# Half of each w3 and w_out block moved from the sync queue to ScalarE's queue

## The chip, the cores and the metric

The kernel runs on one NeuronCore of a Trainium2 chip. Five engines work side by side, each through its own instructions in order: TensorE (PE, matrix products), VectorE (DVE), ScalarE (ACT), GpSimd (POOL) and SyncE (SP). SP computes nothing here; it issues transfers between the device memory and the core's own memory. ScalarE can issue such transfers too, as instructions among its computing ones. The engines meet only at semaphores: an instruction that needs another engine's result, or a transfer's, waits for a count, and everything behind it on its own engine waits with it.

The metric is the device time of one execution in microseconds (us). The median of three runs of the kernel before is 259.25 us (258.74 to 259.34).

## The reference

Attention with a polynomial sketch (4 batches, 4 heads, 1088 positions, 32 dimensions, sketch size 8) feeds a multiplicative feed-forward block over 4352 tokens of width 128 with 1024 inner columns. All inputs are float64.

```python
def phi(x):
    a = np.einsum('rd,bhsd->bhsr', S1, x)
    b = np.einsum('rd,bhsd->bhsr', S2, x)
    return np.einsum('bhsi,bhsj->bhsij', a, b).reshape(*x.shape[:-1], r * r)
q_p, k_p = (phi(q), phi(k))
kv = np.einsum('bhsf,bhsd->bhfd', k_p, v)
z = np.sum(k_p, axis=2)
num = np.einsum('bhsf,bhfd->bhsd', q_p, kv)
den = np.einsum('bhsf,bhf->bhs', q_p, z)[..., None] + 1e-06
x = (num / den).transpose(0, 2, 1, 3).reshape(B * S, H * D)
a = x @ w1
b = x @ w2
out = (a * b @ w3) @ w_out
```

## The kernel before, in words

The tokens are worked in eight groups of 512 (g0 to g7, two to a batch) and a rest of 256 (gr). For each group the queries are sketched and multiplied with the batch's key and value sums; the result is xT, a tile of 128 x 512. The feed-forward block then runs over eight chunks c of the inner 1024 columns: a product with w1 into the bank a_ps (step g.ca, line 1432), a copy of it by ScalarE into ffa (g.cc, line 1437), a product with w2 into b_ps (g.cb, line 1442), VectorE's product ab of the two (g.cm, line 1448), and the product of ab with w3o, summed over the chunks into ps_o (g.co, line 1455).

w3 and w_out are folded first: w3o = w3 @ w_out, in eight row blocks of 128 (steps f0 to f7, lines 465 to 477). The float64 words are turned into float32 on the core. The weights come in eleven blocks, steps w0 to w10: w0 and w1 hold w1 and w2, w2 is all of w_out, w3 to w10 are the eight row blocks of w3. Each has the steps

- load (line 386): 1 MB of raw words into one of three raw buffers; for w2 to w10 in four transfers of 256 KB, quarter t filling partitions 32t to 32t + 31;
- m and c (lines 421 and 226 by way of the helper top_of): two passes of ScalarE over all 128 partitions of the raw tile, so each block's first pass needs all four quarters;
- j (line 434, VectorE) and a (line 439, GpSimd or VectorE): the two halves are joined.

A row block is then transposed (f.t, line 467, VectorE), multiplied with w_out (f.m, line 473, TensorE) and copied into w3o (f.o, line 477, ScalarE).

The order of all steps is written out by hand in the string ORDER, lines 59 to 112. Each engine's instructions are chained in that order (lines 1514 to 1518), so a step's place in the string fixes what stands ahead of it on the engine that carries it out. The engines run asynchronously: SP, which only issues, can be far ahead of the others in the string, held only by its semaphores. A load waits until its raw buffer has been read by ScalarE. Each transfer also signals one of eight completion counters, which are taken in turn, so a transfer waits until the one eight places earlier has landed.

The buffers of each kind are assigned by hand (SLOTS). The eight banks of the kind "b" are shared by the matrix products; a product into a bank waits until the bank's last reader is done.

Places in ORDER of some of the loads (each line is a piece of the string):

```python
q0.pc0 q0.p12 k1.kT0 q0.dn k1.rest0 q0.pt1 warm10 w3.load q0.de k0.kvm
...
q1.xT g0.3a w2.load k1.kp1 q3.max w4.load w2.m w2.c g0.1c
...
w9.m w9.c g1.7m g1.1m v1.loadr q2.p12 q2.dn w8.load v1.load
...
q3.C1 q2.de w5.load q2.rc q2.bs k1.kvc g0.7c q3.At g0.7m k1.kqt f3.m q3.Ct f3.o k1.kq w5.m
...
f2.o w10.load w10.m w7.c
```

In the first, q0.pc0 is a pT copy of ScalarE. In the last, the conversion w10.m is the very next step behind w10.load.

Of the kernel before, what the change touches and what calls it, by code (L numbers as in the profile page):

```python
# [45 lines left out]
WARM = [6] + [2] * 10 + [1] * 24  # L46

BY_PE = ()

POOL = set("""  # L50
    k0.Nf k0.Nh k0.rest1 k1.kp0 k1.kp1 k2.kp0 k3.kp0 q0.p12 q0.phi0 q1.al q1.p12 q1.p2 q2.p12 q2.p2
# [63 lines left out]
def bview(t, free):  # L115
    return bass.AP(tensor=t.tensor, offset=t.offset, ap=[list(t.ap[0])] + [list(d) for d in free])


def make_steps(ctx, tc, q, k, v, S1, S2, moe_w1, moe_w2, moe_w3, moe_w_out, out):
    nc = tc.nc  # L120
    dve, act, pe, pool, sp = nc.vector, nc.scalar, nc.tensor, nc.gpsimd, nc.sync
    B, H, S, D = q.shape
# [15 lines left out]
    def step(name):  # L138
        def keep(f):
            assert name not in steps, name  # L140
            steps[name] = f
            return f
        return keep

    def on(name):
        return pool if name in POOL else act if name in ACTS else dve
# [10 lines left out]
    def sb(tag, shape, dtype=F32, bufs=1, name=None):  # L157
        return place(work, tag, shape, dtype, bufs, name or tag)
# [66 lines left out]
    def top_of(dst, hi):  # L225
        act.activation(dst, hi.bitcast(F32), ACT.Prelu, scale=2.0 ** -112, alpha=-2.0 ** 32)  # L226
# [153 lines left out]
    raw, w3c, w3T = {}, {}, {}  # L380
    NW = 3 + NC

    def conv(n):
        x = {}

        @step(f"w{n}.load")
        def _():
            raw[n] = sb("raw", [128, 1024], I64)
            if n < 2:
                for i, w in enumerate((moe_w1, moe_w2)):  # L390
                    sp.dma_start(raw[n][:, i * 512:(i + 1) * 512], w[:, n * 512:(n + 1) * 512])
            elif n == 2:
                for t in range(4):
                    sp.dma_start(raw[n][t * 32:(t + 1) * 32],
                                 bass.AP(tensor=moe_w_out.tensor, offset=moe_w_out.offset + t * 256 * DM,
                                         ap=[[DM, 32], [32 * DM, NC], [1, DM]]))
            elif n - 3 in BY_PE:
                sp.dma_start(raw[n], moe_w3[(n - 3) * 128:(n - 2) * 128])
            else:
                for t in range(4):  # L400
                    sp.dma_start(raw[n][t * 32:(t + 1) * 32],
                                 bass.AP(tensor=moe_w3.tensor, offset=moe_w3.offset + (n - 3) * 128 * DF + t * 256,
                                         ap=[[DF, 32], [32 * DF, 4], [1, 256]]))


        def shape(x, by, turn):
            if n - 3 not in BY_PE:
                return bview(x, [[by, 1024]])
            return bview(x, [[(32 if turn else 256) * by, 4], [(128 if turn else 32) * by, 8], [by, 32]])

        words = lambda i: shape(raw[n].bitcast(I32)[:, i:], 2, False)

        @step(f"w{n}.c")
        def _():
            x["c"] = sb("cv_c", [128, 1024], bufs=2)
            top_of(shape(x["c"], 1, True), words(1))

        @step(f"w{n}.m")
        def _():
            x["m"] = sb("cv_m", [128, 1024], I32, bufs=2)  # L420
            act.mul(shape(x["m"], 1, True), words(0).bitcast(U32), 2.0 ** -29)  # L421

        def made():
            if n < 2:
                x["d"] = w12[:, n].rearrange("p i c -> p (i c)")
            elif n == 2:
                x["d"] = wo.rearrange("p c d -> p (c d)")
            else:
                x["d"] = w3c[n - 3] = sb("w3c", [128, 1024], bufs=2)
            return x["d"].bitcast(I32)  # L430

        @step(f"w{n}.j")
        def _():
            on(f"w{n}.j").tensor_scalar(made(), x["c"].bitcast(I32), 3, None, ALU.logical_shift_left)  # L434

        @step(f"w{n}.a")
        def _():
            d = x["d"].bitcast(I32)
            on(f"w{n}.a").tensor_tensor(d, d, x["m"], ALU.add)  # L439
# [6 lines left out]
    def fold(ko):  # L446
        t = {}

        if ko in BY_PE:
            for half in range(2):  # L450
# [37 lines left out]
    def rest_ap(src, b):  # L488
        return bass.AP(tensor=src.tensor, offset=(b * H * S + SM) * D, ap=[[D, SR], [S * D, H], [1, D]])

    def k_loads(b):
        @step(f"k{b}.zero")
        def _():
            k_sb[b] = sb("k", [128, H, NK, D], bufs=2)
            pool.memset(k_sb[b][other(b), :, NJ], 0.0)

        def main(heads):
            h0, n = heads
            (act if b == 0 else sp).dma_start(bview(k_sb[b][:, h0], [[NK * D, n], [1, NJ * D]]),
                          bass.AP(tensor=k.tensor, offset=(b * H + h0) * S * D,  # L500
                                  ap=[[NJ * D, 128], [S * D, n], [1, NJ * D]]))

        if b == 0:
            for i in range(2):
                step(f"k{b}.load{i}")(lambda i=i: main((2 * i, 2)))
        else:
            step(f"k{b}.load")(lambda: main((0, H)))

        @step(f"k{b}.loadr")
        def _():  # L510
            sp.dma_start(k_sb[b][own(b), :, NJ], rest_ap(k, b))

        @step(f"v{b}.zero")
        def _():
            v_sb[b] = sb("v", [128, H, NK, D], bufs=2)
            pool.memset(v_sb[b][other(b), :, NJ], 0.0)

        @step(f"v{b}.load")
        def _():
            if b == 0:  # L520
                sp.dma_start(bview(v_sb[b], [[NK * D, H], [1, NJ * D]]),
                             bass.AP(tensor=v.tensor, offset=b * H * S * D,
                                     ap=[[NJ * D, 128], [S * D, H], [1, NJ * D]]))
            else:
                for t in range(4):
                    sp.dma_start(bview(v_sb[b][t * 32:(t + 1) * 32], [[NK * D, H], [1, NJ * D]]),
                                 bass.AP(tensor=v.tensor, offset=b * H * S * D + t * NJ * D,
                                         ap=[[32 * D, 32], [S * D, H], [1, NJ * D]]))

        @step(f"v{b}.loadr")  # L530
        def _():
            sp.dma_start(v_sb[b][own(b), :, NJ], rest_ap(v, b))

        if b:
            @step(f"kh{b}.load")
            def _():
                n = 32 * D
                k_by[b] = sb("kh", [128, n])
                for h in range(H):
                    sp.dma_start(k_by[b][h * 32:(h + 1) * 32],  # L540
                                 bass.AP(tensor=k.tensor, offset=(b * H + h) * S * D, ap=[[n, 32], [1, n]]))

# [1006 lines left out]
```

## Time and profile before

| | |
|---|---|
| median of three runs | 259.25 us |
| the profiled execution | 260.99 us, span 259.2 us |
| TensorE busy | 249.1 us, 96% |
| VectorE busy | 163.8 us, 63% |
| ScalarE busy | 97.1 us, 37% |
| GpSimd busy | 62.4 us, 24% |
| transfers issued | 120 on SP, 2 on ScalarE (the first k loads) |
| w3 blocks | 32 transfers of 256 KB, median 6.9 us from issue to landing |
| w_out | 4 transfers of 256 KB, median 7.9 us |

The span is the time from the first to the last instruction that the profile shows; what lies around it belongs to the execution's own time. Busy times are sums over the span; a stage in which an engine never rests can hide in a low share. "Idle before" in a row is the time for which the engine waited ahead of that row, and the name behind the arrow is what ended the wait. A product in float32 is shown as two instructions, so "x2" is one tile.

### The profile page before, as it was taken

The page shows a single profiled execution, that of the slowest core. Times are in us where ns is not written, and L with a number is a line of the kernel's source. Part 1 is how long each engine was busy: PE and PEld are TensorE (multiplying, and loading weights), DVE is VectorE, ACT ScalarE, POOL GpSimd, SP SyncE. Part 2 cuts the span into 40 slices and gives each one's busy share as a digit, 9 for nine tenths or more (in the row PEclk, how much of TensorE's full clock was granted, in tenths as well). Part 3 has the DMA queues.
Part 4 walks back from the last instruction along what each step waited for, and adds up shares of the span by engine and source line. Part 5 has one row for each costly group of instructions (what it writes and reads, how often), then busy time and mean ns, then how long its engine had stood idle before and what let it go on. Part 6 is the DMA issues. An engine that isn't in the chain of part 4 may idle for free.

```text
span 259.2 us, 5896 instructions
## 1 busy us (share of the span) xinstructions
PE 249.1 (96%) x2457; PEld 136.8 (53%) x2457; DVE 163.8 (63%) x360; ACT 97.1 (37%) x182; POOL 62.4 (24%) x88
## 2 busy tenths in 40 slices
PE   2989999999999899999999999999999999999995
PEld 0667864456564454676455444544444445455554
DVE  3769799798989986997895966241414533341430
ACT  2765476956445590312233337221031201031000
POOL 3523426490436408303520050000001000000000
PEclk9979999999999999999999999999999999999999
DMA  6997499956949963003000001600020000010035
GB/s 184 299 271 181 143 217 215 230 111 147 210 114 230 214 175 81 3 0 90 1 3 3 0 3 29 97 1 0 1 39 0 3 0 0 10 31 3 0 52 90
DMA packets 32314, 22.53 MB, mean 87 GB/s; under 512 B 21408, under 2 KB 26784, under 8 KB 32288
## 3 DMA queue, kind: packets, MB, share of 16 engines
q1 hardware_dynamic: 31744, 21.64, 37.2%
q10 hardware_dynamic: 544, 0.52, 0.6%
q8 instruction: 19, 0.31, 0.5%
q14 instruction: 7, 0.06, 0.1%
HBM read 19.93 MB, written 2.23 MB: 85 GB/s over the span
## 4 chain that ended last, share of the span: by engine, by line
PE 89%; DVE 5%; DMA 2%; SPq 1%; issue 0%
PE b_ps L1442 22%; PE ps_o L1455 21%; PE a_ps L1432 21%; PE ps_w3o L473 6%; PE idle_ps L218 4%; DMA k<-in_k_dram 2%; PE ps_g L599 2%; PE ps_ac L1278 2%; PE ps_x L1392 2%; PE ps_kv L698 2%; PE ps_or L1462 1%; PE ps_ab L642 1%; DVE RC L167 1%; DVE ab L1448 1%; DVE q_m L177 1%; PE ps_xt L1179 1%
## 5 line engine op out<-in xcount | busy, mean ns | idle before, releaser
L1448 DVE TENSOR_TENSOR ab<-ffa,b_ps 128x512 f32<-128x512 f32 (+1 forms) x72 | 44.6, 645 | 48.9 <-PE b_ps L1442 41.9
L1437 ACT COPY ffa<-a_ps 128x512 f32<-128x512 f32 (+1 forms) x72 | 38.5, 565 | 84.4 <-PE a_ps L1432 81.3
L1442 PE MATMUL b_ps<-xT,w 128*128 128x512 f32 (+1 forms) x144 | 67.0, 569 | 0.0
L1432 PE MATMUL a_ps<-xT,w 128*128 128x512 f32 (+1 forms) x144 | 65.2, 568 | 0.0
L1455 PE MATMUL ps_o<-ab,w3o 128*128 128x512 f32 x128 | 61.3, 592 | 0.0
L1432 PEld LDWEIGHTS a_ps<-xT,w 128*128 128x128 f32 x144 | 27.0, 190 | 29.5 <-issue 24.9
L1442 PEld LDWEIGHTS b_ps<-xT,w 128*128 128x128 f32 x144 | 26.9, 190 | 28.9 <-issue 24.2
L1455 PEld LDWEIGHTS ps_o<-ab,w3o 128*128 128x128 f32 x128 | 24.0, 190 | 24.7 <-issue 23.2
L439 POOL TENSOR_TENSOR w3c<-w3c,cv_m 128x1024 int32<-128x1024 int32 x8 | 19.1, 2386 | 26.4 <-DVE w3c L434 15.0
L218 PE MATMUL idle_ps<-zeros 128*128 128x512 bf16 x50 | 16.0, 428 | 4.8 <-DVE zeros L190 4.8
L1373 POOL TENSOR_TENSOR ph<-s_al,s_bs 128x1024 f32<-128x1024 f32 (+1 forms) x5 | 9.9, 1990 | 43.6 <-DVE s_bs L1363 43.6
L473 PEld LDWEIGHTS ps_w3o<-wo,w3T 128*128 128x128 f32 x128 | 15.2, 192 | 4.5 <-DVE w3T L467 2.1
L473 PE MATMUL ps_w3o<-wo,w3T 128*128 128x128 f32 x128 | 15.5, 276 | 1.3 <-DVE w3T L467 1.3
L1471 DVE STREAM_TRANSPOSE oT<-ps_o 128x512 f32<-128x512 f32 x8 | 5.7, 711 | 13.8 <-PE ps_o L1455 13.7
L226 ACT ACTIVATE cv_c<-raw 128x1024 f32<-128x1024 f32 x11 | 12.8, 1166 | 0.0
L421 ACT ACTIVATE cv_m<-raw 128x1024 int32<-128x1024 uint32 x11 | 12.6, 1156 | 0.0
L218 PEld LDWEIGHTS <-zeros 128*128 128x128 bf16 x50 | 5.3, 110 | 10.7 <-DVE zeros L190 4.8
L1403 ACT COPY xT<-ps_x 128x128 f32<-128x128 f32 (+2 forms) x20 | 4.7, 323 | 16.5 <-PE ps_x L1392 14.2
L1330 POOL TENSOR_TENSOR s_al<-s_hl 128x128 f32<-128x128 f32 (+2 forms) x3 | 1.5, 499 | 35.1 <-DVE s_hl L1325 35.1
L467 DVE STREAM_TRANSPOSE w3T<-w3c 128x1024 f32<-128x1024 f32 x8 | 9.9, 1235 | 0.0
L1381 DVE STREAM_TRANSPOSE pT<-ph 128x1024 f32<-128x1024 f32 (+1 forms) x7 | 8.1, 1157 | 2.8 <-POOL ph L1373 2.7
L177 DVE TENSOR_REDUCE k_m<-k 128x1 f32<-128x1152 f32 (+1 forms) x5 | 5.4, 1092 | 5.4 <-DMA k<-in_k_dram 5.4
(241 smaller groups left out, 291.3 us busy)
## 6 DMA issues: line engine op xcount, KB each, us to landing
raw<-in_moe_w_dram SPq DMA_DIRECT2D x32, 256.0 KB, 6.9
qh<-in_q_dram SPq DMA_DIRECT2D x4, 544.0 KB, 5.2
out_dram<-oT SPq DMA_DIRECT2D x34, 64.0 KB, 2.0
raw<-in_moe_w_dram SPq DMA_DIRECT2D x4, 512.0 KB, 8.3
k<-in_k_dram SPq DMA_DIRECT2D x3, 512.0 KB, 6.2
kh<-in_k_dram SPq DMA_DIRECT2D x12, 128.0 KB, 7.4
v<-in_v_dram SPq DMA_DIRECT2D x12, 128.0 KB, 6.2
raw<-in_moe_w_out_dram SPq DMA_DIRECT2D x4, 256.0 KB, 7.9
```

The source lines that it names most:

```text
L218: pe.matmul(t, zeros, bview(zeros, [[0, 4], [1, 128]]), start=True, stop=True)
L226: act.activation(dst, hi.bitcast(F32), ACT.Prelu, scale=2.0 ** -112, alpha=-2.0 ** 32)
L421: act.mul(shape(x["m"], 1, True), words(0).bitcast(U32), 2.0 ** -29)
L439: on(f"w{n}.a").tensor_tensor(d, d, x["m"], ALU.add)
L467: dve.transpose(w3T[ko].rearrange("p s (i r) -> p s i r", r=32), bview(w3c[ko], [[32, NC], [256, 4], [1, 32]]))
L473: pe.matmul(t["o"], w3T[ko][:, c], wo[:, c], start=c == 0, stop=c == NC - 1)
L1373: on(nm(f"phi{u}")).tensor_mul(x, bview(s["al"][:, u * g], [[r, g], [1, r], [0, r]]), bview(s["bs"][:, u * g], [[r, g], [0, r], [1, r]]))
L1432: pe.matmul(x["a"][:, :w], w_of(0, c), xT[g][:, c0:c0 + w], start=True, stop=True)
L1437: act.copy(x["s"][:, :w], x["a"][:, :w])
L1442: pe.matmul(x["b"][:, :w], w_of(1, c), xT[g][:, c0:c0 + w], start=True, stop=True)
L1448: dve.tensor_mul(ab_sb[g, c][:, c0:c0 + w], x["s"][:, :w], x["b"][:, :w])
L1455: pe.matmul(o_ps[g], w3o[:, c], ab_sb[g, c], start=c == 0, stop=c == NC - 1)
```

## The change

The four quarters of each block from w2 to w10 are issued in the order 0, 2, 1, 3. Quarters 2 and 3 are issued by ScalarE, quarters 0 and 1 by SP. The load steps keep their places in ORDER, so on ScalarE the two issues stand behind the ScalarE work of the steps ahead of the load and before the ScalarE work of the steps behind it. The loads of v (from batch 1 on) and of k by heads (kh) take the same new order of quarters, and stay on SP. Nothing else is different.

```diff
+QUARTERS = (0, 2, 1, 3)
...
             elif n == 2:
-                for t in range(4):
-                    sp.dma_start(raw[n][t * 32:(t + 1) * 32],
+                for t in QUARTERS:
+                    (act if t > 1 else sp).dma_start(raw[n][t * 32:(t + 1) * 32],
                                  bass.AP(tensor=moe_w_out.tensor, offset=moe_w_out.offset + t * 256 * DM,
                                          ap=[[DM, 32], [32 * DM, NC], [1, DM]]))
...
             else:
-                for t in range(4):
-                    sp.dma_start(raw[n][t * 32:(t + 1) * 32],
+                for t in QUARTERS:
+                    (act if t > 1 else sp).dma_start(raw[n][t * 32:(t + 1) * 32],
                                  bass.AP(tensor=moe_w3.tensor, offset=moe_w3.offset + (n - 3) * 128 * DF + t * 256,
                                          ap=[[DF, 32], [32 * DF, 4], [1, 256]]))
...
-                for t in range(4):
+                for t in QUARTERS:
                     sp.dma_start(bview(v_sb[b][t * 32:(t + 1) * 32], [[NK * D, H], [1, NJ * D]]),
...
-                for h in range(H):
+                for h in QUARTERS:
                     sp.dma_start(k_by[b][h * 32:(h + 1) * 32],
```

## The prediction

> **What bounds the kernel now.** I read the page's shares and the chain that ended last, then the timelines of ScalarE, the sync queue and VectorE beside each other, then the landing times.
>
> ```profile
> PE 249.1 (96%) x2457; PEld 136.8 (53%) x2457; DVE 163.8 (63%) x360; ACT 97.1 (37%) x182; POOL 62.4 (24%) x88
> ...
> DMA  6997499956949963003000001600020000010035
> ...
> PE 89%; DVE 5%; DMA 2%; SPq 1%; issue 0%
> ```
>
> TensorE is busy 96% of the span and 89% of the chain: time is won only where TensorE waits, and lost wherever it is made to wait. The DMA row (tenths of 6.5 us slices) is at 9 from 32 to 52 us. ScalarE's 37% is an average; its rows at the places where moved loads are to stand (start, length, work, idle before):
>
> ```profile
> 43.06 0.59 ACT L1208 COPY xT<-ps_x 128x512 f32<-128x512 f32 x1 [1.50 <-PE ps_x L1203]
> 43.54 1.15 ACT L421 ACTIVATE cv_m<-raw 128x1024 int32<-128x1024 uint32 x1
> 44.58 1.16 ACT L226 ACTIVATE cv_c<-raw 128x1024 f32<-128x1024 f32 x1
> 45.65 0.56 ACT L1437 COPY ffa<-a_ps 128x512 f32<-128x512 f32 x1
> ...
> 69.90 1.15 ACT L226 ACTIVATE cv_c<-raw 128x1024 f32<-128x1024 f32 x1
> 72.44 0.37 ACT L728 COPY kvc<-ps_kv 128x256 f32<-128x256 f32 x1 [1.39 <-PE ps_kv L705]
> ...
> 76.07 1.16 ACT L421 ACTIVATE cv_m<-raw 128x1024 int32<-128x1024 uint32 x1
> ...
> 93.12 0.42 ACT L477 COPY w3o<-ps_w3o 128x128 f32<-128x128 f32 x2
> 93.42 1.17 ACT L421 ACTIVATE cv_m<-raw 128x1024 int32<-128x1024 uint32 x1
> ...
> 97.03 0.58 ACT L1437 COPY ffa<-a_ps 128x512 f32<-128x512 f32 x1
> 108.12 1.25 ACT L171 ACTIVATE kk<-k,k_g 128x1152 f32<-128x1152 f32 x1 [10.51 <-DVE k_g L579]
> ```
>
> From 43.06 to 52.98 ScalarE works without a gap, while it is free for 10.5 us after 97.61. Now the sync queue's issues of the same loads, and landings counted from an issue's start:
>
> ```profile
> 29.95 1.98 SPq L394 DMA_DIRECT2D raw<-in_moe_w_out_dram  x4
> 59.40 1.97 SPq L401 DMA_DIRECT2D raw<-in_moe_w_dram  x4
> ...
> raw<-in_moe_w_dram SPq DMA_DIRECT2D x1, 256.0 KB, 4.4
> raw<-in_moe_w_dram SPq DMA_DIRECT2D x1, 256.0 KB, 5.9
> ...
> k<-in_k_dram ACTq DMA_DIRECT2D x2, 256.0 KB, 3.1
> ```
>
> The w_out block (step w2.load) leaves at 29.95, and its conversion reads it on ScalarE at 43.54: 13.6 us ahead. The sync queue can do that because it only issues and runs far ahead of the computing engines. The 4.4 and 5.9 are the second and fourth quarter of the group issued from 59.40 (step w8.load), nearly alone in its queue. The two k loads on ScalarE's queue have a median of 3.1 and 2.9 for the first, so 3.3 for the second. w_out's four have a median of 7.9 and 9.7 for the last.
>
> **The change, part by part.** Nine blocks lose two of four issues on SP and gain two on ScalarE: 18 issues of about 0.45 us (the w_out issues' median; w3's is 0.43), 8.1 us in all.
>
> *SP: nothing gained.* SP's long waits end with outputs (94.9 us for L1410), and no transfer of these blocks ends a wait on the chain. The new order of quarters in the v and kh loads stays on one queue, and their readers need all four: nothing. In the built program each transfer takes one of eight completion counters in turn and waits for the transfer eight places before it, so SP now waits for some of ScalarE's. The tightest is kh2.load's last quarter, 45.82 before: it waits for a w_out quarter that lands at 43.65 + 4.4 = 48.1 and holds w9.load and v1.loadr behind it. With kh's median of 7.4 it lands at 55.5, and its reader, the kT transpose of 55.40, is itself 5 us late by then: hidden.
>
> *Place w3.load: 0.1 us.* It now follows the pT copy, which ends at 27.35. Two issues take 0.9 against 0.56 idle before 27.92: 0.34 late. The ps_kz product at 28.71 starts 0.27 after that copy: 0.1 remains. The data is read at 34.22; the second issue starts at 27.80 and lands at 33.7 by the 5.9 row. By 9.7 it would land at 37.5, 3.3 late, of which ScalarE's 0.7 us wait before 40.48 hides a part: upper bound 2.6.
>
> *Places w2.load and w4.load: 5.3 us.* In the built program the four issues stand behind the xT copy (ends 43.65) and straight before the conversion of w_out. The second starts at 43.65 + 0.45 = 44.10, and the conversion needs it landed. I take 4.4: 48.5 instead of 43.54, so ScalarE is 5.0 us late. (Bounds: the k loads' 3.3 gives 3.9 late; w_out's median of 7.9 gives 8.5; a landing in the busy ring, 9.7, gives 10.2. The 4.4 is nearest because the sync queue has by then half the backlog of before.) Behind the waiting conversion stand the ffa copy of 45.65 and all that follows. That copy ends at 46.21; VectorE's product needs it at once:
>
> ```profile
> 46.24 1.28 DVE L1448 TENSOR_TENSOR ab<-ffa,b_ps 128x512 f32<-128x512 f32 x2 [0.91 <-ACT ffa L1437]
> ...
> 95.64 0.69 DVE L434 TENSOR_SCALAR w3c<-cv_c 128x1024 int32<-128x1024 int32 x1 [0.31 <-ACT cv_c L226]
> ...
> 101.76 0.78 DVE L1289 STREAM_TRANSPOSE ay_A<-ps_ac 128x256 f32<-128x256 f32 x2 [2.38 <-PE ps_ac L1278]
> ```
>
> and TensorE's fifth a_ps tile of the row of twelve at 43.32 (43.32 + 4 x 0.86 = 46.76), which needs its bank, starts 0.55 after it. So VectorE is 5.0 late and TensorE 4.45. Next w6.load puts 0.9 us more on ScalarE (its data is read 8 us later): 5.9 late at the ffa copy ending 52.98, which the a_ps tile at 53.62 follows by 0.64: TensorE is 5.26 late. From there to 86 TensorE and VectorE wait for each other with gaps under 0.7 us, so the delay stays: 5.3 with rounding; bounds 4.1 (3.9 + 0.9 - 0.64) and 10.5.
>
> *Place w9.load: nothing.* It falls before ScalarE's 3.06 us idle at 56.84.
>
> *Places w8.load and w5.load: nothing, barely* (all in times of this trace, shifted alike). Four issues after the conversion ending at 71.05: 1.8 us against 1.39 idle, 0.4 late at kvc, whose product follows 0.57 later. The fourth starts at 72.4 and lands at 78.3 by the 5.9 row; its reader stands at 76.07, 2.2 late. The xT copies behind it are then 1.9 late, of which 0.32 idle and 0.87 before the a_ps tile at 80.23 come off; about 1.0 reaches TensorE and vanishes in its 1.25 us gap at 86.40. If it lands after 9.7 us, 3.5 reaches that gap and 2 remain.
>
> *Place w7.load: nothing.* Its two issues fall before 1.79 us idle, and its reader is 7 us behind.
>
> *Place w10.load: 2.6 us.* Here too the conversion is the very next instruction. The second issue starts at 93.54 + 0.45 = 93.99, lands at 98.4: ScalarE 5.0 late against 93.42. VectorE's shift at 95.64 follows ScalarE directly, is 5.0 late, and wins 2.38 back at 101.76. TensorE needs the ffa copy ending 97.61 for its ps_ac products at 100.05: 2.44 to spare, 2.6 late; VectorE agrees. (Bounds: 3.3 gives 3.9 late and 1.4; 9.7 gives 10.3 and 7.8.) The 10.5 us idle then clears ScalarE's backlog, but not TensorE's.
>
> *The sum.* 0.1 + 5.3 + 0 + 2.6 = 8.0 us. The profiled execution took 260.99 us with a span of 259.2 us; with 8.0 it would be 269.0. The median of the unprofiled runs is 259.25, 1.7 below it; there I forecast **267.3 us**. Adding only the lower bounds gives 0 + 4.1 + 1.4 = 5.5, 264.8.
>
> *Two queues.* The quarters of the group at 59.40 were issued 0.47 apart and landed 1.2 us apart (59.99 + 4.4, 60.94 + 5.9: 2.4 for two): the transfer sets the pace, not the issue. No row has two queues loaded at once. The Trainium skill, "DMA: Bandwidth & Descriptors", section "Issuing engines are not separate DMA queues", says that transfers of all issuers run on the same 16 engines, and a second issuer saves only issue time. By that nothing is won; if the queues added up instead, the landings would go to the 3.3 row and the time to 264.8.
>
> **Rivals.**
>
> *Short landings.* Every ScalarE transfer lands like the k loads: 264.8, or 263.4 if w10 hides wholly. For it: that queue is empty. Against: those ran when nothing else was loaded.
>
> *Long landings.* ScalarE's transfers share the engines with the sync queue's (9 tenths up to 52 us). By w_out's 7.9: 0.1 + 8.7 (8.5 + 0.9 - 0.64) + 1 + 6.0 (8.5 - 2.44) = 15.8, 275; halfway between, 271.
>
> *A halved clock.* TensorE stands still 4.4 us near 47. The windows show it once:
>
> ```profile
> 14.00:17.50 3.50, 3.15 (x39) 2.53 (x36) 2.75 (x14) 2.75 (x6) 1.54 (x4) 0.64 0.90 294
> 17.50:22.00 4.50, 4.50 (x46) 2.79 (x46) 3.19 (x13) 0.96 (x2) 1.27 (x3) 0.90 0.96 218
> ```
>
> The granted clock (third from the end) fell to 0.64 and 0.90, after thin use of TensorE: 0.36 x 3.5 + 0.10 x 4.5 = 1.7 us of clock. Here TensorE would be 4.45 + 1.7 = 6.15 late instead of 5.26: 268.1. Against: the 1.25 us gap at 86.40 cost no clock. "TensorE: Matmul & The Clock Gate", Part 1, of the Trainium skill, puts an idle window of about 3.4 us at half clock; no gap of that length behind warm work is in this trace.
>
> *Not slower.* ScalarE's issues go out before the copies ahead of them finish, as SP's do. It decides if w_out's quarters leave 4.4 us before 43.54, by 39.1; ScalarE's wait just before begins only at 41.56. Then nothing is late: 259.3. Against: the k loads in this trace stand first in their queue, so no row shows one overtaking.
>
> **How the numbers follow.** Forecast 0.47, halved clock 0.13, short 0.15, long 0.20, not slower 0.05. Slower is 0.95; the last 0.05 I split 0.03 within 0.3% (what a measurement here can tell) and 0.02 faster, since nothing on the chain is shortened. The range starts at 263.4 (all short landings) and ends at 272, leaving out the not slower case and about half of the long one.
>
> **What would show it.** ScalarE's conversion of w_out waits for a DMA of raw for 3 to 5 us near 46 us, and the last block's near 103; ACT rows then name DMA as releaser, which no conversion does now. TensorE shows a gap of some 4 us near 47 and one of 2 to 3 near 107. SP's issues change and its outputs move with the end. Wrong would be: conversions that don't wait (issues run ahead), a wait of 8 us (shared ring), or a gap at TensorE that VectorE's slack swallows.

## The result and the profile after

Before, 259.29 us (median of four runs beside the changed kernel, 258.74 to 260.37); after, **271.38 us** (median of four, 270.7 to 272.64). The ratio is 1.047, interval 1.044 to 1.050: 12.1 us slower. The forecast was 267.3 with a range of 263.4 to 272. The profiled execution took 272.64 us, its span is 270.9.

The front part quotes the order around the last block as `f2.o w10.load w10.m w7.c`; in the code a step of VectorE stands between, `f2.o w10.load k2.kp1 w10.m w7.c w7.j`. On ScalarE w10.m is still the next instruction behind w10's issues. It also calls all inputs float64; q, k and v are float32 (a transfer of 544 KB holds 4 x 1088 x 32 numbers of four bytes), and only the weights and sketches are wider.

The page of the changed kernel: busy time, TensorE's row, the clock's and the transfers' (40 slices of 6.8 us), and the shares of the chain that ended last.

```profile
PE 253.0 (93%) x2457; PEld 137.4 (51%) x2457; DVE 165.9 (61%) x360; ACT 97.1 (36%) x182; POOL 62.3 (23%) x88
...
PE   3989999099999989899999999999999999999995
...
PEclk9979999689999999999999999999999999999999
DMA  6993799843777993010200000430020000020025
```

TensorE's row has a 0 in the eighth slice (47.4 to 54.2 us), and its clock is at 6 there. What ended the waits (us in total, times, longest):

```profile
DVE ab L1450 <- ACT ffa L1439: 13.5, 4, 7.6
ACT cv_m L423 <- DMA raw<-in_moe_w_dram: 11.4, 2, 6.9
DVE w3c L436 <- ACT cv_c L228: 6.4, 3, 4.9
PE a_ps L1434 <- ACT ffa L1439: 6.3, 1, 6.3
```

Two conversions (cv_m) now wait for transfers, 11.4 us together; before, none did. ScalarE's timeline shows which (start, length, work, idle before):

```profile
43.54 0.59 ACT L1210 COPY xT<-ps_x 128x512 f32<-128x512 f32 x1 [1.50 <-PE ps_x L1205]
43.60 1.07 ACTq L396 DMA_DIRECT2D raw<-in_moe_w_out_dram  x2
45.07 1.01 ACTq L403 DMA_DIRECT2D raw<-in_moe_w_dram  x2
51.06 1.12 ACT L423 ACTIVATE cv_m<-raw 128x1024 int32<-128x1024 uint32 x1 [6.94 <-DMA raw<-in_moe_w_dram]
...
53.08 0.59 ACT L1439 COPY ffa<-a_ps 128x512 f32<-128x512 f32 x1
...
102.15 0.91 ACTq L403 DMA_DIRECT2D raw<-in_moe_w_dram  x1
...
106.58 1.13 ACT L423 ACTIVATE cv_m<-raw 128x1024 int32<-128x1024 uint32 x1 [4.49 <-DMA raw<-in_moe_w_dram]
```

These are w_out's conversion, 6.94 us late (forecast 5.0), and the last block's, 4.49 late (5.0). (The row at 51.06 names a transfer of w3, but the counter that reached its count just before, at 50.90, is that of w_out's last quarter.) The copy ffa that stood at 45.65 now starts at 53.08, and TensorE stands 6.33 us for it. The windows (us, busy time of PE, PEld, DVE, ACT, POOL, then the granted clock, transfers' share, GB/s) show the clock behind it:

```profile
46.00:50.00 4.00, 1.40 (x4) 0.33 (x2) 0.13 (x2) 0.00 (x0) 2.34 (x1) 0.99 1.05 215
50.00:54.00 4.00, 0.28 (x1) 0.28 (x2) 0.30 (x1) 2.94 (x4) 0.00 (x0) 0.50 0.67 153
54.00:58.00 4.00, 4.00 (x7) 1.73 (x8) 3.74 (x5) 2.60 (x5) 0.00 (x0) 0.66 0.85 171
```

From 49.89 to 56.72 us TensorE ran at half clock. In the kernel before, the clock is full in this stage; a halved clock stood among the forecast's rivals.

In what follows, lateness is told by marks: the start of the same ScalarE instruction in two traces, less the difference that both had already before the first moved load (it varies by up to 3 us between executions). Against the trace with every quarter on the sync queue, the changed kernel is 8.1 us late from 63 us on and 11.2 at the end.

### The profile page after: what moved, and what is told of

It reads as the page before. It is cut to its first block, busy times and chain, and to the rows that moved or that the text cites. A ratio compares the mean times of both kernels' runs of the same rounds, so it can differ in the third digit from the quotient of the medians.

```text
span 270.9 us, 5904 instructions
## 1 busy us (share of the span) xinstructions
PE 253.0 (93%) x2457; PEld 137.4 (51%) x2457; DVE 165.9 (61%) x360; ACT 97.1 (36%) x182; POOL 62.3 (23%) x88
## 4 chain that ended last, share of the span: by engine, by line
PE 75%; DMA 9%; DVE 8%; ACT 4%; SPq 1%; issue 1%; ACTq 0%
PE b_ps L1444 18%; PE a_ps L1434 18%; PE ps_o L1457 18%; DMA raw<-in_moe_w_dram 7%; PE ps_w3o L475 4%; PE idle_ps L220 3%; DMA k<-in_k_dram 2%; PE ps_ac L1280 2%; PE ps_g L601 2%; PE ps_x L1394 2%; ACT cv_c L228 2%; PE ps_kv L700 2%; PE ps_or L1464 1%; ACT cv_m L423 1%; ACT ffa L1439 1%
## 5 line engine op out<-in xcount | busy, mean ns | idle before, releaser
L1434 PE MATMUL a_ps<-xT,w 128*128 128x512 f32 (+1 forms) x144 | 67.0, 580 | 6.3 <-ACT ffa L1439 6.3
L220 PE MATMUL idle_ps<-zeros 128*128 128x512 bf16 x50 | 16.7, 446 | 4.7 <-DVE zeros L192 4.7
L423 ACT ACTIVATE cv_m<-raw 128x1024 int32<-128x1024 uint32 x11 | 12.6, 1154 | 11.6 <-DMA raw<-in_moe_w_dram 11.4
L436 DVE TENSOR_SCALAR w3c<-cv_c 128x1024 int32<-128x1024 int32 x8 | 5.5, 685 | 6.4 <-ACT cv_c L228 6.4
```

The lines of the kernel that those rows point to most:

```text
L220: pe.matmul(t, zeros, bview(zeros, [[0, 4], [1, 128]]), start=True, stop=True)
L1434: pe.matmul(x["a"][:, :w], w_of(0, c), xT[g][:, c0:c0 + w], start=True, stop=True)
```

## The experiments

### Which blocks cost, and does the order

Five kernels, each with only some blocks' upper quarters on ScalarE: none, w_out (2), w4 (4), w10 (10), and all others (3, 5, 6, 7, 8, 9).

```diff
+ON_ACT = (2,)
...
-                    (act if t > 1 else sp).dma_start(raw[n][t * 32:(t + 1) * 32],
+                    (act if t > 1 and n in ON_ACT else sp).dma_start(raw[n][t * 32:(t + 1) * 32],
```

> Every quarter back on the sync queue, in the changed order 0, 2, 1, 3. If the queue is what costs (both theories below): no change, 259.3 us, at most 0.5 more. Rival: the order itself delays the last quarter of kh and v or of the blocks; then part of the 12.1 us stays, 262 or more.

> Only the two upper quarters of w_out go by ScalarE; w4, and all else, by the sync queue. Theory A (the landing took 6.95 us since the sync queue's backlog, in flight from 39 to 51 us, shares the 16 DMA engines with it): the backlog is still there, with two quarters of w4 more in it, so the last quarter of w_out lands 6 to 8 us after ScalarE issues it, the conversion waits so long, TensorE stands over 5 us, its clock is halved for some us: 266.5 to 268. Theory B (w4's two quarters behind it on ScalarE's own queue held it up): it lands in 4.4 us as the rows of before have it, ScalarE is 4.4 us late, TensorE less than 4: 263 to 264.5.

> Only the two upper quarters of w4 go by ScalarE, issued near 43.6 us since w_out's are not ahead of them; its conversion stood at 47.44 us before. Theory A: they land 6 to 8 us after the issue, at 50 to 51.5, and that conversion is 2.5 to 4 us late; of this TensorE has one or two products to go on with, so 1.5 to 3.5 us: 261 to 263. Theory B: 4.4 us, landed by 48.4, 1 us late at ScalarE and nothing at the end: 259.3 to 260.

> Only the two upper quarters of w10, the last block, go by ScalarE. Both theories: the landing takes 4.3 us as in the changed kernel (the sync queue has little in flight there), the conversion waits 4.5 us: 2.6 (the term of the forecast) to 3.2 us (the delay read between the two traces), 261.9 to 262.5. If the delay of 0.9 us on VectorE behind it came only together with the first stall, 2.2: 261.5.

> The upper quarters of w3 and w5 to w9 go by ScalarE, those of w_out, w4 and w10 by the sync queue. The forecast put these places at 0.1 us in all, and the three other places alone measured +8.3, +0.1 and +3.0: 259.3 to 260. Rival (the places cost nothing only while TensorE is late from w_out's stall): 260.5 or more.

| on ScalarE | us | ratio to before (interval) |
|---|---|---|
| none, new order only | 259.14 | 0.9992 (0.9976 to 1.0009) |
| w_out | 267.94 | 1.0336 (1.0302 to 1.0371) |
| w4 | 259.71 | 1.002 (0.9993 to 1.0046) |
| w10 | 262.63 | 1.0124 (1.0086 to 1.0162) |
| w3, w5 to w9 | 259.34 | 0.9991 (0.9969 to 1.0013) |

The parts add up to 3.36 + 0.20 + 1.24 - 0.09 - 0.08 = 4.6%, against 4.7% for the whole. The order costs nothing, six blocks cost nothing, and w_out alone is some 70% of it. Theory B falls: w4's quarters are gone from ScalarE's queue and the wait stays (ScalarE's and TensorE's waits, w_out alone):

```profile
ACT cv_m L424 <- DMA raw<-in_moe_w_out_dram: 6.8, 1, 6.8
PE a_ps L1435 <- ACT ffa L1440: 6.1, 1, 6.1
```

It also settles a trap in the changed kernel's chain, which runs through a quarter of w4 that landed at 52.78, just ahead of the copy ffa at 53.08. In both kernels that copy starts 2.0 us after w_out's conversion (48.24 and 50.25; 51.06 and 53.08): w4 is not what it waited for. For w4 alone theory A misses: it had a landing of 6 to 8 us and 261 to 263. The two quarters, issued at 41.16 and 41.54, landed after 4.4 and 4.7 us, at 45.58 and 46.24; their conversion at 46.31 waits for nothing, and the end is no later than can be told.

The landing of each transfer is read from its completion counter. For w_out alone on ScalarE:

```
transfer            queue    issued  landed
w4, fourth issue    sync     35.65   41.42
w6, first           sync     36.51   42.59
w6, second          sync     36.86   43.74
w6, third           sync     37.87   44.99
w_out, quarter 2    ScalarE  40.90   47.41
w_out, quarter 3    ScalarE  41.28   48.09
```

The sync queue's quarters land some 1.15 us apart. ScalarE's come behind all of those issued earlier. The packets show the same: from 42.5 to 43.5 us 122 of the sync queue's moved and 4 of ScalarE's, from 44 to 48.2 us 488 of ScalarE's and none of the sync queue's. With w4 alone less stood in front: the sync queue's last quarter landed 2.6 us after ScalarE's first issue (43.74 against 41.16), here 4.1 us (44.99 against 40.90). Behind that last landing, the second ScalarE quarter took 2.5 and 3.1 us more.

The changed kernel came to much the same wait in another way. A transfer steps its counter sixteen times, the last time when all of it has landed. Of the steps of the last w_out quarter, issued at 43.95, fourteen had come by 48.89, 4.9 us after the issue; the last two came at 49.88 and 50.90. In this execution the last step is behind the fourteenth by 3.9 us for the first w_out quarter (issued at 31.63), and still by 2.0 us for the last. With w_out alone it is behind by 0.7 us for the last quarter, and by at most 0.1 for the four sync quarters of the table. So with w_out alone the whole quarter waited behind others; in the changed kernel, with less in front, most of it was there after 4.9 us, and a part that lagged came 2.0 us later. The lag was there before w4's quarters were issued (45.07), so they did not cause it; why that part lagged, no run shows.

### Take the backlog away

w6 leaves the sync queue, and goes whole by ScalarE behind w_out's conversion; w_out's place is the same.

```diff
-g0.4a w6.load kh2.load
+g0.4a kh2.load w6.load
...
-(act if t > 1 and n in ON_ACT else sp)
+(act if t > 1 and n in ON_ACT or n == 6 else sp)
```

> As the run with w_out alone on ScalarE, its issues at the same place, but w6, whose three first quarters stood ahead of them in the engines, goes whole by ScalarE behind the conversion of w_out. Theory A: the two quarters of w_out then stand behind w4 alone (landed at 41.42) and some of kh: landed at 44.5 to 45.5 in place of 48.09, wait of 3.3 to 4.3 us in place of 6.8; TensorE stands some 3 us, with less or no time at half clock: 263 to 264.5. Theory B: w6 doesn't matter, 267.5 to 268.5.

264.44 us, ratio 1.020 (1.013 to 1.026): 3.5 us less than with w6 ahead. ScalarE's timeline of this run:

```profile
40.56 1.11 ACTq L397 DMA_DIRECT2D raw<-in_moe_w_out_dram  x2
45.63 1.12 ACT L424 ACTIVATE cv_m<-raw 128x1024 int32<-128x1024 uint32 x1 [4.49 <-DMA raw<-in_moe_w_out_dram]
```

And TensorE's, at the product that waits for ScalarE's copy:

```profile
48.29 3.56 PE L1435 MATMUL a_ps<-xT,w 128*128 128x512 f32 x4 [3.87 <-ACT ffa L1440]
```

The last quarter, issued at 40.95, landed at 45.48: 4.5 us, against 6.8 with three quarters of w6 ahead of it. Theory A holds in the landing (44.5 to 45.5) and in the time (263 to 264.5), at the upper edge of both; the wait, 4.49 us, is longer than its 3.3 to 4.3. Only the last quarter of w4 and two of kh were then left in front (landed by 42.32). So three quarters of w6 in front are 2.3 of the 6.8 us.

### Move the place in ScalarE's order

w_out alone on ScalarE, its two issues earlier: once behind w1's conversion, with four more copies and the copy xT between them and their reader, once ahead of w3's conversion.

```diff
-w1.j k2.load
+w1.j k2.load w2.load
...
-w2.load k1.kp1
+k1.kp1
```

```diff
-k1.gram4 warm22 w3.c w3.m
+k1.gram4 warm22 w2.loada w3.c w3.m
...
+        if n == 2:
+            @step("w2.loada")
+            def _():
+                raw[n] = sb("raw", [128, 1024], I64)
+                for t in (2, 3):
+                    act.dma_start(raw[n][t * 32:(t + 1) * 32],
```

> As the run with w_out alone on ScalarE (267.94 us; the last quarter issued at 41.28, landed at 48.09, while the sync queue's w4 and w6, issued by 38.2, landed one after the other from 37.85 to 44.99, some 1.15 us apart), but its two issues stand two copies and two pT copies earlier in ScalarE's order, near 36.4 us. Theory A, now sharper: the engines serve the quarters in the order in which they were issued, whatever the queue. Behind w4 and the first quarter of w6 (landed at 42.59) the two land near 43.7 and 44.9, 3 to 3.5 us late: 262 to 263.5. Theory B (a landing of 4 to 5 us of its own): by 41.3, in time: 259.3 to 260.

> The same two issues still earlier, right behind the copy xT of the first head group, near 32 to 34 us, before the sync queue issues w4. By theory A they are then ahead of w4 in the engines, land by 40, the conversion doesn't wait: 259.3, at most 260. By a theory that a transfer from ScalarE's queue is slower in itself, or stands back behind the sync queue's, the wait stays above 2 us: 262 or more.

259.38 us (ratio 0.9991, 0.9965 to 1.0016) and 258.90 (0.9979, 0.9959 to 1.0000): both gain back the whole 8 us, and neither beats the kernel before by what can be told. For the second theory A is right: the two quarters landed at 37.28 and 38.49, behind the sync queue's two of w_out at 34.73 and 36.13. For the first it named 262 to 263.5 from an issue at 36.4, and that premise was wrong (ScalarE's timeline, first of the two):

```profile
31.30 0.58 ACT L1200 COPY xT<-ps_xs 128x512 f32<-128x512 f32 x1 [3.96 <-PE ps_xs L1196]
31.58 0.34 ACTq L397 DMA_DIRECT2D raw<-in_moe_w_out_dram  x1
31.78 1.23 ACT L229 ACTIVATE cv_c<-raw 128x1024 f32<-128x1024 f32 x1
31.95 0.48 ACTq L397 DMA_DIRECT2D raw<-in_moe_w_out_dram  x1
32.92 2.16 ACT L424 ACTIVATE cv_m<-raw 128x1024 int32<-128x1024 uint32 x2
34.98 0.19 ACT L766 COPY krab<-ps_krab 128x64 f32<-128x64 f32 x1
35.08 1.15 ACT L229 ACTIVATE cv_c<-raw 128x1024 f32<-128x1024 f32 x1
36.13 1.21 ACT L1440 COPY ffa<-a_ps 128x512 f32<-128x512 f32 x2
...
41.10 1.15 ACT L424 ACTIVATE cv_m<-raw 128x1024 int32<-128x1024 uint32 x1
```

Both issues stand behind the cv_c of 35.08 in the written order, and went out at 31.58 and 31.95, the first ahead of five instructions that had nothing left to wait for, the second ahead of four. What held the issues back is the last instruction before them that waited, the copy xT of 31.30. The quarters landed by 38.16 and the conversion at 41.10 waits for nothing. So the two runs do not differ in what they test, and the first said nothing on theory A.

### Keep the clock

w_out alone on ScalarE, with 24 and then 20 products of zeros between TensorE's g1.2a and g1.1a, in a bank that is free there.

```diff
-WARM = [6] + [2] * 10 + [1] * 24
+WARM = [6] + [2] * 10 + [1] * 24 + [24]
...
-g0.2m g1.2a g1.2c g1.1a
+g0.2m g1.2a warm35 g1.2c g1.1a
```

> As the run with w_out alone on ScalarE (267.94 us, 8.3 to 8.7 over before; TensorE stood 6.14 us, then half clock from near 50 to 57), with 24 multiplications of zeros (0.216 us each at full clock, 5.2 us) put on TensorE where it stands, between the products g1.2a and g1.1a; they lie in the gap. If the halved clock is what makes 8.3 out of a stall of 6.1 to 6.2: the clock stays at 1.0 and 2 us come back, 265.5 to 266.3. If the clock only slows work that would wait for ScalarE anyway: 267.5 to 268.3.

> As the run with 24 zero products in the gap, with 20 (4.3 us). There the clock stayed at 1.0 and VectorE and ScalarE were 2.4 us less late by 61 us than without them, but TensorE stood 1.14 us at 123.47 between two products of the last batch's Gram matrix with no releaser in the profile, and the time was 267.73. If that gap belongs to the place where the 48 added instructions pushed the program, and not to the clock: with 40 added it is gone or elsewhere, the clock is at 1.0, 265.3 to 266.5. If the full clock is paid back in some other way whatever the count: 267.3 to 268.

267.73 us (1.0312, 1.0287 to 1.0337) and 266.99 (1.023, 1.016 to 1.030), against 267.94 without. By the time alone the first says that the clock doesn't matter: it lies in that rival's 267.5 to 268.3. The second lies in neither of its bands. The traces say otherwise. One window of w_out alone (the clock is third from the end):

```profile
52.00:54.00 2.00, 2.00 (x4) 0.92 (x3) 1.97 (x4) 0.99 (x1) 0.00 (x0) 0.50 0.91 223
```

The same window of the run with 24:

```profile
52.00:54.00 2.00, 1.88 (x5) 0.93 (x6) 1.90 (x4) 2.00 (x4) 0.00 (x0) 1.00 0.75 225
```

By 61 us the marks are 9.1 us late without the zeros, 6.7 with 24 and 6.2 with 20, though the conversion waited much the same (6.76, 7.07, 6.51). Up to there the halved clock is 2.4 to 3.0 us of w_out's price.

How much of the half clock falls behind TensorE's release gives the same, as an estimate. With w_out alone TensorE started again at 50.89 and had half clock until 56.44: half of these 5.6 us is 2.8 lost. In the changed kernel it started at 53.72 and had half clock until 56.72: 1.5. With w6 behind, all 3.4 us of half clock came after the start at 48.29: 1.7. The marks, less the conversion's wait and the 0.55 us that TensorE had to spare, leave 2.9, 1.7 and 1.9.

Then the chain of the run with 24 shows a place where TensorE stood with no releaser:

```profile
122.78 0.68 PE ps_g L602 x34
123.47 1.14 issue
124.61 0.37 PE ps_g L602 x5
```

With 20 it stood 1.59 us at 122.75 in the same run of products; w_out alone has no such row, and the marks lose 1.4 and 1.8 us there, so that only some 1 us of the gain is left at the end. The second run's expectation, that it goes or moves elsewhere, failed. In both, one packet of the profile's instruction queue moves in the microsecond or two before it, which suggests that the 48 and 40 added instructions made TensorE wait for its own program there. Such a packet moves near there with w_out alone too, without a gap, so that is argued and not shown: what makes this gap stays open.

### The last block's 0.9 us

The forecast had 2.6 for w10; w10 alone costs 3.0 (the marks: 3.2). VectorE was 2.2 us late up to 106 us; its timeline then, with w10 alone on ScalarE:

```profile
106.50 2.01 DVE L1339 TENSOR_TENSOR s_pr<-s_hl 128x256 f32<-128x256 f32 x1
108.43 0.71 DVE L1343 TENSOR_TENSOR s_pr<-s_al,s_hl 128x128 f32<-128x128 f32 x1
```

In the run with all on the sync queue these took 0.41 and 0.28. GpSimd's kp ran from 106.28 to 108.22 beside the first; without the delay it ended 0.7 us ahead of it. So kp's product was moved behind GpSimd's own s_pr sum:

```diff
+            if b == 2:
+                @step("k2.kp0x")
+                def _():
+                    k_phi(f["kp", 0], f["abs"][:, 0, :, 0], f["abs"][:, 0, :, 1], pool)
...
-q3.p12 f7.m
+q3.p12 k2.kp0x f7.m
```

> As the run with w10 alone on ScalarE (262.63 us), where VectorE's product s_pr (128x256) took 2.01 us in place of 0.41 while GpSimd's kp (1.94 us) ran beside it; here GpSimd's first kp of batch 2 is done behind its own s_pr sum. If that overlap is the 0.9 us between the 2.2 us seen on TensorE at ps_ac and the 3.0 to 3.2 measured: s_pr falls to at most 1.1 us (kpr, 0.8 us, may still lie beside it), 261.5 to 262.1. If not: 262.4 to 262.9, s_pr still near 2.

VectorE's timeline of this run:

```profile
106.12 0.41 DVE L1345 TENSOR_TENSOR s_pr<-s_hl 128x256 f32<-128x256 f32 x1
106.45 0.28 DVE L1349 TENSOR_TENSOR s_pr<-s_al,s_hl 128x128 f32<-128x128 f32 x1
...
108.23 0.97 DVE L1363 SCALAR_TENSOR_TENSOR s_rc<-s_d 128x16 f32<-128x16 f32 x1
```

The overlap is what stretched s_pr: it is back at 0.41, and now s_rc (0.17 before) runs beside kp (107.22 to 109.17) and takes 0.97, to kp's end. The time is 261.93 us, ratio 1.0108 (1.0087 to 1.0129), and lies in the band expected; but the interval overlaps that of w10 alone, and this profiled execution had 3.4 us of halved clock from 100.5 on and is 3.8 us late by the marks, against 3.2. What the move gives back in time is not settled.

### Everything early

The whole change, with w_out and w4 behind k2's load and w10 behind w7's; the sync queue's order is as before.

```diff
-w1.j k2.load
+w1.j k2.load w2.load w4.load
...
-w8.m w7.load q3.sm
+w8.m w7.load k3.loadr w10.load q3.sm
...
-q3.sh k3.loadr f2.o w10.load k2.kp1
+q3.sh f2.o k2.kp1
```

> The whole change, upper quarters of w3, w_out and every later block by ScalarE, but three loads stand earlier in the written order: w_out and w4 right behind the load k2 (in ScalarE's order ahead of four copies instead of right ahead of their reader), w10 right behind w7's load. The sync queue's order is as before. If the place in ScalarE's order is all that costs: no wait over 0.6 us at any conversion, 259.0 to 260. If the second queue costs by itself: 261 or more.

262.95 us, ratio 1.015 (1.011 to 1.019): 8.4 us of 12.1 come back. The first expectation misses, in the time and in its waits (the last block's conversion waits 1.14 us). The time lies in the second's band, 261 or more; what costs of the second queue is, for the most part, not its landings but the issues that have to wait (ScalarE's timeline of this run):

```profile
35.77 2.62 ACTq L404 DMA_DIRECT2D raw<-in_moe_w_dram  x2
38.44 1.07 ACT L1440 COPY ffa<-a_ps 128x512 f32<-128x512 f32 x2 [2.01 <-PE ps_ph L1160]
...
83.76 5.00 ACTq L404 DMA_DIRECT2D raw<-in_moe_w_dram  x2
88.80 1.15 ACT L1250 ACTIVATE q<-qT,q_m 128x1024 f32<-128x1024 f32 x1 [4.35 <-DMA raw<-in_moe_w_dram]
```

Each transfer waits for the one eight places before it. The second issue of w4 waited for a quarter of w_out that landed at 38.06, and the second of w10 for a quarter of w7 that landed at 88.42. An issue that waits on ScalarE holds all of ScalarE's work behind it: 2.0 us (the copy at 38.44 starts as the issue ends, though its row names TensorE) and 4.35 us. On the sync queue the same waits hold only transfers.

## Why the prediction was right or wrong

**Bound, direction, and the zeros: right.** TensorE was the bound, and it lost what the two conversions waited. The places w3, w9, w8 and w5, and w7 came to nothing, as did the order and the sync queue's lighter load: 259.34 and 259.14. The 0.1 for w3 can't be told from nothing. As forecast, the last quarter of kh2 had to wait for a quarter of w_out (landed at 48.78; issued at 48.80), and the marks show no delay from it. Of the signs, the last block's wait of 4.49 us came as told; w_out's wait and TensorE's gap near 47 were longer, and near 107 no row of TensorE waits for more than 0.90 us: there the lateness is spread over the ps_ac products, six of which take 1.32 us.

**Places w2.load and w4.load: 5.3 forecast, 8.1 by the marks in the changed kernel.** The term that was too small is "I take 4.4", the landing of a quarter nearly alone, chosen "because the sync queue has by then half the backlog of before". It took 6.95 us. For most of the transfer the choice was near: fourteen of sixteen steps came within 4.9 us. The rest is the part that lagged by 2.0 us, for which the forecast had no term. With w_out alone, and so w4's last quarter and three of w6 in front, the landing took 6.8 us as a whole, and 4.5 with w6 out of the way. With 6.94 late in place of 5.0, and the 0.55 to spare that the forecast found, TensorE is 6.4 late, which is its 6.33 us gap.

The Trainium skill, "DMA: Bandwidth & Descriptors", section "Issuing engines are not separate DMA queues", says that all issuers' transfers run on the same 16 engines and interleave there. The prediction took from it that nothing is won, and priced the sharing in its long landings. No run here beats the kernel before by what can be told, which agrees. But with w_out alone the two queues hardly interleaved, and the late issue stood behind what was issued before, 47.41 behind 44.99.

The remaining 1.7 us of the 8.1 fits the halved clock, given as a rival that costs 1.7 us, 0.9 of them net. That the 1.7 came out is luck: it was taken from thin work at the kernel's start, while here a gap of 6.3 us brought 6.8 us of half clock, of which 3.0 lay behind TensorE's release. With w_out alone it is 2.4 to 3.0 us by the runs with zeros. So two of the named rivals, long landings and the clock, both came true in part, and the forecast's own price alone did not. The range held the time since it reached towards them; that it also had room for the lagging part, which no term names, is luck.

w6's issues, which the sum put at 0.9 us more of lateness, cost nothing: they went out at 51.23 and 52.14, while ScalarE was computing, and the conversions and copies from 51.06 to 55.8 follow each other without a gap.

**Place w10.load: 2.6 forecast, 3.0 measured.** The steps behind it were right: landing 4.3 (4.4), ScalarE 4.5 late (5.0), 2.2 left at TensorE. What it lacked is GpSimd: the delay moved VectorE's s_pr into GpSimd's kp. The Trainium skill, "SBUF — State Buffer", section "SBUF: two separate sides", says that VectorE, with both inputs in SBUF, and GpSimd share a pair of ports that one of them holds for a whole instruction. The rows of 2.01 and 0.97 us agree: they end 0.3 and 0.03 us behind kp. How much of the 3.0 this is stays open.

**A slip in a bound.** For w8 and w5 the forecast lets 3.5 us reach TensorE's gap if the landing takes 9.7 us, and 2 remain. By its own steps the reader is then 6.0 us late, some 4.5 reach the gap and 3.3 remain; with 5.9 it is 0.7, not 1.0. The sum of 8.0 doesn't use it, and the places cost nothing.

**"Not slower": wrong for this place, right as a mechanism.** Issues do run ahead of the work written before them, by 3.1 us in the run with w_out earlier (31.95 against 35.08). At the change's place the copy xT, which waits for TensorE until 43.54, stands straight in front.

**The sum.** 8.7 (w_out alone by its ratio) + 3.2 (w10) + 0.3 (the rest, not told from nothing) = 12.2, against 12.1 measured; forecast 8.0. By the marks of the changed kernel it is 8.1 and 3.1, 11.2 in all.

## What to carry to other kernels

A load that is issued from a computing engine's order went out here only when the last waiting instruction before it was released, so its place must be counted from that wait to its reader, and against all transfers that any queue has issued by then, not against a lone transfer's landing. Where the issue itself must wait, for a buffer or for a completion counter, the computing engine's work waits with it: a queue that does nothing else is the place for such loads. When the bounding engine stands, look at its clock behind the gap: here 6 us of standing cost 1.7 to 3 us more by the marks. And a transfer has landed only when its slowest part has: here that part came up to 3.9 us behind the rest.

## What was not expected of the hardware

- ScalarE's transfers overtook its own instructions in the written order: issued at 31.58 and 31.95 us, ahead of work that started at 31.78 to 35.08.
- 3.87 us of standing gave 3.4 us of half clock, and 6.1 to 6.3 us gave 6.8. But with kp later 3.4 us came after gaps of only 0.18 and 0.88 us, where w10 alone had a gap of 0.89 and none: the length of one gap does not tell.
- Added work on TensorE in a gap was paid elsewhere: 1.14 and 1.59 us without a releaser, some 75 us later, behind 48 and 40 more instructions.
